# Folding once more over the sequence: even and odd output rows from batch 2 on, in a fused attention and Fourier-mixing kernel

## The chip, the cores and the metric

The kernel runs on one core of a Trainium2 chip. The metric is device microseconds of one execution. TensorE is called PE in the profile, its weight loads PEld, VectorE DVE, ScalarE ACT, GpSimd POOL, and the queue of SyncE SP.

## The reference

Inputs are q, k, v of 8 batches x 12 heads x 448 tokens x 64, and two weights of 768 x 3072 and 3072 x 768, all fp32. Cut to what matters:

```
scores = (1/8) * q @ k^T                 # per batch and head
attn   = max(scores, 0)**2 / 448
x      = attn @ v                        # 8 x 448 x 768 with the heads side by side
mixed  = real(fft(fft(x, axis=1), axis=2))    # over 448 tokens, then over 768 channels
u      = x + mixed
un     = (u - mean(u)) / sqrt(var(u) + 1e-6)  # over the channels
out    = u + max(un @ w1, 0) @ w2
```

## The kernel before

Each batch goes through attention, Fourier mixing, normalization and the feed-forward product (FFN). All of it is written as generators that yield an engine, an estimated duration and what they wait for; a planner (`Streams.run`, L93) takes the step that can start first by its estimates, and so writes a fixed order of instructions for each engine. Semaphores between the engines are put in afterwards, from what each instruction reads and writes. An engine that is later on the chip than in the plan makes the others wait; nothing is reordered at run time.

**Attention** (`attention`, L568) makes the scores of one head pair and quarter of the keys (L645), ACT takes the relu (L670), DVE or ACT squares it (L682, L685), and four such quarters times v give `x` transposed: 128 channels by 448 tokens in PSUM (L627). There are six such blocks m = 0..5 per batch.

**Folding** (`fold`, L489). `leave` scales a block into SBUF as bf16 in two halves: tokens 0..223 from column 0 of `xTc[m]`, and tokens 447..224 backwards from column XH + 1 (XH = 256). So the sum and the difference of the two halves (L535, L537; 225 columns each) are what the cosine and the sine of the transform over the tokens need: each half of the output rows follows from 225 folded tokens in place of 448. Block m and block m + 3 are then combined in the same way over the channels (L546, L549, 450 columns each) into `Bs` and `As`. Each `leave` also starts a DMA transpose (`turn_x`, L555) on SP that gives `xn`, x with tokens on the partitions.

**Mixing** (`mix`, L1096; `mix_rows`, L925). The folded blocks are the stationary side of the channel products with a cosine and sine table `chan` (L1112): folded tokens in two chunks TC of 128 and 97, each 12 matmuls of 193 columns, so 24 per batch. ACT and DVE copy the result to `pc` (L1128). Then the products over the tokens make output rows in two half batches SC, 0..127 and 128..239 (`ch`): for each of cosine and sine two matmuls of 385 columns, one per chunk, accumulate in PSUM (L933), four per half batch. Their sum and difference (L942, L944) give the output row s and the mirrored row 448 - s.

```
for t in range(2):
    for i, (n0, n1) in enumerate(TC):
        nc.tensor.matmul(pq[:n, t, 0:KN], lhsT=seq[:n1 - n0, t, i, s0:s1],
                         rhs=pcs[i][0][:n1 - n0, t, 0:KN], start=(i == 0), stop=(i == 1))
```

Rows and mirrored rows get x added (L960, L962, on DVE and POOL), statistics (L969), and normalization to `un` (L985, L988). `store_rows` (L1012) writes u and un to DRAM: the rows by a plain DMA on SP, the mirrored rows by an indirect DMA on POOL with the row numbers in `back`. `turns` (L1042) fetches `un` transposed for groups of tokens that the FFN takes (384, 512, 384, then nine of 256).

**FFN** (`ffn`, L1275): L1344 is the first product, L1318 and L1316 its relu, L1369, L1395 and L1475 the second product, L1330 the addition to u. PE interleaves FFN work of earlier groups with attention and mixing of later batches; from about 480 us on only FFN is left.

Batches 0 and 1 go partly on paths of their own (`first_tail`, L708; `turn_rows`, L897). `build_dft` (L280) makes the table `seq` over the tokens, `mirrors` (L260) a reversal matrix and the row numbers, on POOL.

Of the kernel before, what the change touches and what calls it, by code (L numbers as in the profile page):

```python
# [140 lines left out]
def mm(n):  # L141
    return n / 2400 + 0.006
# [22 lines left out]
def kernel(  # L165
# [9 lines left out]
    nc = tc.nc  # L175
# [52 lines left out]
    rev = const.tile([128, 128], BF16, name="rev")  # L228

    back = [const.tile([128, 1], mybir.dt.int32, name=f"back{i}") for i in range(2)]  # L230
    warm = work.tile([128, 512], BF16, name="warm", tag="warm", bufs=1)
    xTc = [const.tile([128, 2 * XH], BF16, name=f"xT{m}") for m in range(MC)]

    drow = const.tile([128, 8], FP32, name="drow")
    early_hid = work.tile([128, 6 * KH], FP32, name="early", tag="hT", bufs=1)
# [22 lines left out]
            nc.gpsimd.memset(x[:, XH + NS:2 * XH], 0.0)  # L258

    def mirrors():  # L260
        nc.gpsimd.memset(rev, 0.0)
# [11 lines left out]
    seq = const.tile([128, 2, 2, SX], BF16, name="seqm")  # L273
    nseq = work.tile([128, 2, SX], BF16, name="nseq", tag="qs", bufs=1)
    chan = [const.tile([128, 2, 2 * KH], BF16, name=f"chan{m}") for m in range(3)]

# [39 lines left out]
            dft_ready.t = chan_ready[m].t = e + LATENCY["DVE"]  # L316


    GRP = 4 * R * HG * Dh * 4
    loads = [[None] * 3 for _ in range(B * NG)]  # L320
    ready = [[Cell() for _ in range(3)] for _ in range(B * NG)]
# [6 lines left out]
    def load_group(i, which=(0, 1, 2)):  # L328

        b, g = divmod(i, NG)  # L330
        hs = slice(g * HG, (g + 1) * HG)
        for x, (nm, src) in enumerate((("q", q), ("k", k), ("v", v))):
            if x not in which:
                continue
            if b == 0 and x < 2:
                e = yield need("POOL", 0.85)
                t = first_qk[x][:R, g]
            else:
                e = yield need("POOL", 0.85, bufs=[BQ[x] if x == 2 else BQ[x][home(i)]])
                t = work.tile([R, HG, 4 * Dh], BF16, name=f"{nm}n",  # L340
                              tag="vn" if x == 2 else f"{nm}n{home(i)}", bufs=3 if x == 2 else 1)
            nc.gpsimd.dma_start(out=t, in_=src[b, hs].rearrange("h (p j) d -> p h (j d)", j=4))  # L342
            loads[i][x] = t.rearrange("p h (j d) -> p j h d", j=4)

            ready[i][x].t = sch.dma(e, GRP, 360e3, "sw") + (1.5 if g else 0.0, 3.0, 14.0, 7.0)[min(b, 3)]
            if i == 0 and x == 1:
                yield need("POOL", 0.7)
                make_identity(nc, ident)
            if i == 0 and x == 2:
                e = yield need("POOL", 1.1)  # L350
                dft_indices()
                indices_ready.t = e + LATENCY["POOL"]
            if i == 2 and x == 2:
                yield need("POOL", 0.75)
                pads()
            if i == NG + 1 and x == 1:
                yield need("POOL", 1.8)
                mirrors()


# [128 lines left out]
    def fold(b, m, F, av, give, av_end):  # L489
# [3 lines left out]

        def leave():

            xa = x[:, 0:HS].rearrange("q (p j) -> q p j", j=4), at[:, 0:R // 2]
            xb = x[:, XH + 1:XH + NS].rearrange("q (p j) -> q p j", j=4), at[:, R - 1:R // 2 - 1:-1, ::-1]
            if b == 0:
                t = yield need("DVE", 2 * dve(HS) + 2 * dve2(NS), [av_end], [BX[m]] + ([BA[m]] if m < 3 else []))
                for out_, in_ in (xa, xb):  # L500
# [1 line left out]
            else:  # L502
                yield need("PE", 0.0, [av_end - LATENCY["PE"]])
                en = "ACT" if sooner(av_end, "ACT", 2 * act(HS), "DVE", 2 * dve(HS)) else "DVE"
                bufs = [BX[m]] + ([BA[m]] if m < 3 else [])
# [25 lines left out]
        f = work.tile([128, 2, NS], BF16, name="fold", bufs=1,  # L531
                      tag=f"diff{m - 3}" if b == 0 and m >= 3 else f"fold{min(m, 3)}")
        if not one:
            e1 = yield need("DVE", dve2(NS), [e1])
        nc.vector.tensor_tensor(f[:, 0, :], x[:, 0:NS], x[:, XH:XH + NS], op=ALU.add)  # L535
# [3 lines left out]
        if b == 0:  # L539
            first_folds.append(f)  # L540
            f_ready[m].t = e1 + LATENCY["DVE"]
        elif m >= 3:
            i = m - 3
            e1 = yield need("DVE", (2 if one else 1) * dve2(2 * NS))
            t = work.tile([128, 2, NS], BF16, name="diff", tag=f"diff{i}", bufs=1)
# [3 lines left out]
            nc.vector.tensor_tensor(F[i], F[i], f, op=ALU.add)  # L549
            As[b].append(F[i])  # L550
            ab_ready[b][i].t = e1 + LATENCY["DVE"]

    xn_taken = [Cell() for _ in range(B)]

# [153 lines left out]
    def first_tail(pcs):  # L708
# [180 lines left out]
        yield from unload(3, "DVE")  # L889
        yield from copy(3, 1, "DVE")  # L890
        tail[0] = 2
        sch.add(turn_rows(uns[0][1], max(t_un[1]), 128, rev[:, 63:127], 0, 64, "DVE", second_un[0]), (1, 1))


# [30 lines left out]
    def mix_rows(b, ch, pcs):  # L925

        s0, s1 = SC[ch]
        n = s1 - s0
        e = yield need("PE", 4 * mm(KN), [pcs[0][1], pcs[1][1]], [BS, BTS])
        pq = BS.take()  # L930
        for t in range(2):
            for i, (n0, n1) in enumerate(TC):
                nc.tensor.matmul(pq[:n, t, 0:KN], lhsT=seq[:n1 - n0, t, i, s0:s1],  # L933
                                 rhs=pcs[i][0][:n1 - n0, t, 0:KN], start=(i == 0), stop=(i == 1))
        if ch == 1:
            BPC.free.append(e)
        e = yield need("ACT", act(KN), [e + LATENCY["PE"]])
# [71 lines left out]
        yield need("SP", 0.0, made_un)  # L1009
        un_ready[b][ch].t = max(c.t for c in made_un)  # L1010

    def store_rows(ch, top, bot, us, nbytes, t, cells):  # L1012

        get = lambda u: u() if callable(u) else u
        s0, s1 = SC[ch]
        w = min(128, HS - s0)
# [5 lines left out]
        nc.gpsimd.indirect_dma_start(  # L1022
            out=bot, out_offset=bass.IndirectOffsetOnAxis(ap=back[ch][:s1 - s0], axis=0),
            in_=get(us[1])[:s1 - s0], in_offset=None)
        cells[2 * ch + 1].t = sch.dma(e, w * D * nbytes) + 1.0

    def u_store(b, ch, us, ut, freed):
        yield from store_rows(ch, utop[b], ubot[b], us, 4, ut, u_stored[b])
        yield need("SP", 0.0, freed)
        for i in range(2):  # L1030
            t = max(u_stored[b][2 * ch + i].t, freed[i].t)
            BU[i][side(b, ch)].free.append(t)
            if b == ONE - 1 and ch == 0:
                u_left[i].t = t

    def n_store(b, ch, t):
        yield from store_rows(ch, ntop[b], nbot[b], [lambda i=i: uns[b][2 * ch + i] for i in range(2)], 2,
                              t, n_stored[b])
        if b > 0:
            BUN[0].free.append(n_stored[b][2 * ch + 1].t)  # L1040
# [55 lines left out]
    def mix(b):  # L1096
# [5 lines left out]
            pps = [(pp, c.t + LATENCY["PE"]) for pp, c in zip(first_pps, first_chan)]  # L1102
        else:
            A, Bm = As[b], Bs[b]
            for n0, n1 in TC:
                n = n1 - n0
                e = yield need("PE", 12 * mm(KH), ab_ready[b] + [dft_ready], [BS])
                pp = BS.take()
                for t in range(2):
                    for kp, Y in enumerate((A, Bm)):  # L1110
                        for m in range(3):
                            nc.tensor.matmul(pp[:n, t, kp * KH:(kp + 1) * KH], lhsT=Y[m][:, t, n0:n1],  # L1112
                                             rhs=chan[m][:, t, kp * KH:(kp + 1) * KH],
                                             start=(m == 0), stop=(m == 2))
                pps.append((pp, e + LATENCY["PE"]))
        for m in range(3):
            BA[m].free.append(e)
        for (n0, n1), (pp, t) in zip(TC, pps):
            n = n1 - n0
# [438 lines left out]
    with tc.manual_schedule():  # L1558
# [11 lines left out]
        sch.add(attentions(), (3, 3))  # L1570
        sch.add(warming(), (9, 9))
        sch.add(weight_sums(), (6, 6))
        sch.add(turns(), (1, 1))
        for slot in range(6):
            sch.add(outputs(slot), (4, 0))
# [32 lines left out]
```

## Time and profile before

| | |
|---|---|
| median of 3 runs | 588.73 us (588.59 to 589.23) |
| profiled execution | 588.36 us, span 586.6 us |
| busy PE, DVE, ACT, POOL | 574.5, 411.2, 324.9, 131.0 us |
| granted TensorE clock | 1.0 throughout |
| channel products L1112 | 24 per batch; batches 2 to 7 start at 159, 214, 279, 339, 401 and 460 us |
| row products L933 | 8 per batch, in two sets of four |

The span is what the profiler saw between the first and the last instruction; the rest of the 588.36 us lies around it. Matmuls are pipelined: the duration of one is longer than the distance between two starts, and it is the distance that counts for throughput. In a group of the page, what follows the bar is its busy time and the mean duration of one, then the idle time of its engine just ahead of them and what ended it.

### The profile page before, as it was taken

Reading aid. Unit: us, or ns where it says so; the run is one execution under the profiler, and the core shown is the slowest. Engines: PE = TensorE matmul, PEld = TensorE weight load, DVE = VectorE, ACT = ScalarE, POOL = GpSimd, SP = SyncE. Lnnn points to the kernel's source line nnn. Section 1 sums busy time; section 2 is a strip of 40 time slices with the busy share of each in tenths; the row PEclk is TensorE's granted clock in tenths of the full one; section 3 lists DMA queues with packets and bytes.
Section 4 is the critical chain, followed back from the end, with each engine's and each line's share of the span. In section 5 each row is a group of like instructions: output and inputs, shape, how many; then the busy total and the mean of one; then the engine's idle time right before and its main releaser. Section 6 shows DMA issues by size and latency. Waiting matters only on the chain.

```text
span 586.6 us, 11549 instructions
## 1 busy us (share of the span) xinstructions
PE 574.5 (98%) x4493; PEld 366.8 (63%) x4498; DVE 411.2 (70%) x979; ACT 324.9 (55%) x501; POOL 131.0 (22%) x181
## 2 busy tenths in 40 slices
PE   8999999999999999999999999999999999999997
PEld 6566556544455465556757677567576786868684
DVE  5977677986688959787897778777887682222222
ACT  5967772787767568655738447466485261404040
POOL 8433021411224114211231124210230120000000
PEclk9999999999999999999999999999999999999999
DMA  9999999787959995999659967885472153121211
GB/s 128 207 210 228 217 209 141 183 123 98 179 101 212 187 143 176 158 153 165 105 146 194 166 147 183 147 124 109 143 184 60 50 186 114 41 85 48 73 37 54
DMA packets 133494, 82.30 MB, mean 140 GB/s; under 512 B 77504, under 2 KB 128608, under 8 KB 133440
## 3 DMA queue, kind: packets, MB, share of 16 engines
q0 software_dynamic: 40320, 34.07, 37.6%
q1 hardware_dynamic: 93120, 47.50, 37.0%
q8 instruction: 35, 0.57, 0.4%
q14 instruction: 19, 0.16, 0.1%
HBM read 62.91 MB, written 26.69 MB: 153 GB/s over the span
## 4 chain that ended last, share of the span: by engine, by line
PE 87%; DVE 6%; ACT 3%; DMA 2%; issue 1%; SPq 1%; POOL 0%; DVEq 0%; ACTq 0%; POOLq 0%
PE psF L1344 35%; PE psF L1475 25%; PE psS L645 6%; PE psF L627 5%; PE psF L1395 4%; PE psF L1369 4%; PE psS L1112 2%; ACT sq L670 2%; DMA qkT<-qkr 2%; PE psS L933 2%; DVE sq L685 1%; PE psS L627 1%; PE psS L732 1%; SPq L1262 1%; PE psS L1087 1%
## 5 line engine op out<-in xcount | busy, mean ns | idle before, releaser
L1344 PE MATMUL psF<-unT,w 128*128 128x256 bf16 (+2 forms) x1723 | 229.6, 290 | 1.9 <-ACT unT L907 0.9
L1344 PEld LDWEIGHTS <-w 128*128 128x128 bf16 x1728 | 165.7, 98 | 62.5 <-issue 13.1
L670 ACT ACTIVATE sq<-psS 112x896 bf16<-112x896 f32 x192 | 163.1, 917 | 60.3 <-PE psS L645 56.8
L1318 ACT ACTIVATE hT<-psF 128x512 bf16<-128x512 f32 (+3 forms) x172 | 86.8, 519 | 109.5 <-PE psF L1344 107.3
L685 DVE TENSOR_TENSOR sq<-sq 112x896 bf16<-112x896 bf16 x173 | 106.7, 634 | 15.8 <-ACT sq L670 14.2
L1475 PEld LDWEIGHTS <-hT 128*128 128x128 bf16 x792 | 76.4, 98 | 54.1 <-issue 5.5
L1330 DVE TENSOR_TENSOR o<-psF,o 128x384 f32<-128x384 f32 x92 | 51.0, 554 | 46.2 <-PE psF L1475 41.4
L1475 PE MATMUL psF<-w,hT 128*128 128x384 bf16 x462 | 81.2, 326 | 0.6 <-DVE o L1330 0.6
L645 PE MATMUL psS<-qkT 64*128 64x448 bf16 (+1 forms) x384 | 51.2, 358 | 2.4 <-ACT sq L670 0.8
L342 POOL DMA_DIRECT2D vn<-in_v_dram x24 | 17.2, 716 | 105.1 <-PE psS L645 100.7
L627 PE MATMUL psF<-sq,vn 112*64 112x448 bf16 x328 | 38.8, 359 | 0.0
L512 DVE TENSOR_SCALAR xT<-psF 128x224 bf16<-128x224 f32 x62 | 21.4, 386 | 24.8 <-PE psF L627 23.4
L960 POOL TENSOR_TENSOR u<-tp,xn 128x385 f32<-128x385 f32 (+1 forms) x14 | 13.6, 973 | 103.6 <-DVE tp L942 81.9
L1475 PE MATMUL psF<-wsum,hT 128*128 128x384 bf16 x198 | 34.8, 326 | 0.0
L645 PEld LDWEIGHTS <-qkT 64*128 64x128 bf16 (+1 forms) x384 | 15.9, 102 | 29.4 <-issue 22.6
L342 POOL DMA_DIRECT2D qn<-in_q_dram x21 | 15.4, 733 | 73.7 <-DVE qkr L435 46.7
L627 PEld LDWEIGHTS <-vn 112*64 112x64 bf16 x384 | 17.6, 109 | 21.1 <-issue 12.7
L969 DVE BATCH_NORM_STATS2 stats<-u 128x6 f32<-128x384 f32 (+1 forms) x56 | 28.7, 540 | 0.3 <-POOL u L960 0.3
L988 ACT ACTIVATE un<-u,nmr,rstd 128x768 bf16<-128x768 f32 (+1 forms) x23 | 23.1, 1024 | 9.3 <-DVE nmr L975 8.3
L1369 PE MATMUL psF<-w,hT 128*128 128x384 bf16 x144 | 24.9, 326 | 0.0
L1395 PE MATMUL psF<-w,hT 128*128 128x384 bf16 x144 | 24.7, 326 | 0.2
L1457 DVE TENSOR_TENSOR s<-hT 128x768 bf16<-128x768 bf16 x11 | 6.1, 555 | 25.7 <-ACT hT L1318 25.5
(148 smaller groups left out, 621.8 us busy)
## 6 DMA issues: line engine op xcount, KB each, us to landing
out_dram<-o SPq DMA_DIRECT2D x56, 192.0 KB
vn<-in_v_dram POOLq DMA_DIRECT2D x24, 224.0 KB, 5.8
qn<-in_q_dram POOLq DMA_DIRECT2D x21, 224.0 KB, 7.9
kn<-in_k_dram POOLq DMA_DIRECT2D x21, 224.0 KB, 6.1
w<-in_moe_w_ch_dram POOLq DMA_DIRECT2D x12, 384.0 KB, 14.6
w<-in_moe_w_ch_dram POOLq DMA_DIRECT2D x4, 1152.0 KB
utop<-u SPq DMA_DIRECT2D x8, 384.0 KB
o<-utop SPq DMA_DIRECT2D x16, 192.0 KB
```

What stands on the lines that cost most here:

```text
L342: nc.gpsimd.dma_start(out=t, in_=src[b, hs].rearrange("h (p j) d -> p h (j d)", j=4))
L627: nc.tensor.matmul(av[h * Dh:(h + 1) * Dh, 0:S], lhsT=vn[:, c, h0 + h, :], rhs=sq[:, h, :], start=(c == 0), stop=(c == 3))
L645: nc.tensor.matmul(sc[:wide, h, 0:S].rearrange("k (c q) -> k c q", c=4), lhsT=flat[ps, k0:k0 + wide], rhs=qT[ps, m % 2], start=True, stop= ...
L670: nc.scalar.activation(r, sc[:R, :, 0:S], AF.Relu)
L685: nc.vector.tensor_tensor(r, r, r, op=ALU.mult)
L969: nc.vector.bn_stats(stats[:n, hf, :], u[:n, hf * (D // 2):(hf + 1) * (D // 2)])
L1318: nc.scalar.activation(hs, ps, AF.Relu)
L1330: nc.vector.tensor_tensor(o, pc[:, 0:DH], o, op=ALU.add)
L1344: nc.tensor.matmul(ph[:, i * N:(i + 1) * N], lhsT=w1_sb[m][hf][:, (jj + i) * 128:(jj + i + 1) * 128], rhs=unT[:, m, 0:N], start=(m == 0), ...
L1369: nc.tensor.matmul(pc[:, 0:DH], lhsT=block(j, c), rhs=w2(j, hf), start=(j == 0), stop=(j == JC - 1))
L1395: nc.tensor.matmul(pc[:, 0:DH], lhsT=block(2 * i + k, c), rhs=weights[i], start=(start and i == 0), stop=(i == KP - 1), skip_group_check=True)
L1475: nc.tensor.matmul(pc[:, 0:DH], lhsT=lhs[i], rhs=rhs[i], start=(start and i == 0), stop=(i == KP - 1), skip_group_check=True)
```

## The change

From batch 2 on (PAR = 2) `leave` writes each half with even tokens first and odd tokens behind them. `halves` replaces the folds: it waits for three blocks m, takes sum and difference over all three at a time (EV = 113 columns each for even and odd tokens), and folds each of these once more, columns 0..56 against 112..56 read backwards (EH = 57): the sum serves the even output rows, the difference the odd ones. The combination of m and m + 3 then runs over all of it in two operations of 1368 columns. In `mix` the stationary side of the channel products is 114 columns (57 for the even, 57 for the odd tokens), one set of 12 matmuls for the sums and one for the differences. In `mix_rows` a half batch is the even or the odd rows, 113 and 112 of them, and each needs one matmul for cosine and one for sine. `halve`, run once, makes the smaller table from `seq` with a selection matrix `order`; two memsets in batch 2 clear a pad column. The stores write every second row. Several tiles share homes: three blocks m lie in one tile, `seq` lies in a work buffer that the folds use later.

```
+    PAR, EV = 2, 113
+    EH = EV // 2 + 1
...
+    xT3 = [const.tile([128, 3, 2 * XH], BF16, name=f"xT{k}") for k in range(2)]
+    xTc = [xT3[m // 3][:, m % 3] for m in range(MC)]
...
+    def halve():
+        yield need("SP", 0.0, [tail_left])
+        e = yield need("PE", mm(2 * SX), [], [BS])
+        pt = BS.take()
+        for t in range(2):
+            nc.tensor.matmul(pt[:2 * EH, t, 0:SX], lhsT=order[0][:EV, 0:2 * EH], rhs=seq[:EV, t, 0, :],
+                             start=True, stop=True)
+        e = yield need("DVE", 1.1, [e + LATENCY["PE"]], [BQR])
+        half_seq[0] = work.tile([128, 2, 2, EV], BF16, name="seqh", tag="warm", bufs=1)
+        nc.vector.tensor_copy(half_seq[0][:2 * EH].rearrange("p t o s -> p t s o"),
+                              pt[:2 * EH, :, 0:2 * EV].rearrange("p t (s o) -> p t s o", o=2))
...
     def fold(b, m, F, av, give, av_end):
...
+        if b >= PAR:
+            x_gone[b].append(gone)
+            sch.add(leave(), (0, 0))
+            if m % 3 == 2:
+                sch.add(halves(b, m // 3), (3, 3))
+            return
...
+    def halves(b, k):
+        x = xT3[k]
+        xa, xb = (x[:, :, at:at + 256].rearrange("q m (o e) -> q m o e", o=2)[:, :, :, 0:EV] for at in (0, XH))
+        e1 = yield need("DVE", dve2(6 * EV) + 0.1 * (b == PAR), x_gone[b][3 * k:3 * k + 3] + [seq_left], [BFS])
+        if b == PAR:
+            nc.vector.memset(x[:, :, EV - 1:EV], 0.0)
+        f = work.tile([128, 3, 2, 2, EV + 1], BF16, name="folds", tag="seqm", bufs=1)
+        nc.vector.tensor_tensor(f[:, :, 0, :, 0:EV], xa, xb, op=ALU.add)
+        e1 = yield need("DVE", dve2(6 * EV))
+        nc.vector.tensor_tensor(f[:, :, 1, :, 0:EV], xa, xb, op=ALU.subtract)
+        f = f.rearrange("q m t o e -> q (m t) (o e)")
+        low = f.rearrange("q c (o e) -> q c o e", o=2)[:, :, :, 0:EH]
+        high = f[:, :, 0:2 * EV].rearrange("q c (o e) -> q c o e", o=2)[:, :, :, EV - 1:EH - 2:-1]
+        for w, op in enumerate((ALU.add, ALU.subtract)):
+            e1 = yield need("DVE", dve2(12 * EH), [], [(BFA, BFB)[k]] if w == 0 else [])
+            if w == 0:
+                Y = work.tile([128, 2, 6, 2, EH], BF16, name="fold", tag=("foldA", "foldB")[k], bufs=1)
+            nc.vector.tensor_tensor(Y[:, w], low, high, op=op)
+        if k == 0:
...
+            return
+        first, second = (y.rearrange("q w c o e -> q (w c o e)") for y in (firsts[b], Y))
+        e1 = yield need("DVE", dve2(24 * EH))
+        t = work.tile([128, 24 * EH], BF16, name="diff", tag="seqm", bufs=1)
+        nc.vector.tensor_tensor(t, first, second, op=ALU.subtract)
+        e1 = yield need("DVE", dve2(24 * EH))
+        nc.vector.tensor_tensor(first, first, second, op=ALU.add)
...
     def mix_rows(b, ch, pcs):
...
-        n = s1 - s0
-        e = yield need("PE", 4 * mm(KN), [pcs[0][1], pcs[1][1]], [BS, BTS])
+        n = s1 - s0 if b < PAR else EV - ch
+        e = yield need("PE", (4 if b < PAR else 2) * mm(KN), [pcs[0][1], pcs[1][1]] + [half_ready] * (b >= PAR),
+                       [BS, BTS])
         pq = BS.take()
         for t in range(2):
+            if b >= PAR:
+                nc.tensor.matmul(pq[:n, t, 0:KN], lhsT=half_seq[0][:2 * EH, t, ch, 0:n],
+                                 rhs=pcs[t ^ ch][0][:2 * EH, t, 0:KN], start=True, stop=True)
+                continue
...
     def store_rows(b, ch, top, bot, us, nbytes, t, cells):
...
-            nc.sync.dma_start(out=top[s0:s0 + w, :], in_=get(us[0])[:w])
+            nc.sync.dma_start(out=top[s0:s0 + w, :] if b < PAR else top[ch::2, :], in_=get(us[0])[:w])
...
     def turns():
-                deps = n[1::2] if half else n[0:3:2][int(r0 >= 128):1 + int(r0 + w > 128)]
+                deps = n[half::2]
...
     def mix(b):
-            for n0, n1 in TC:
-                n = n1 - n0
+            for w, (n0, n1) in enumerate(TC):
+                n = n1 - n0 if b < PAR else 2 * EH
...
-                            nc.tensor.matmul(pp[:n, t, kp * KH:(kp + 1) * KH], lhsT=Y[m][:, t, n0:n1],
+                            nc.tensor.matmul(pp[:n, t, kp * KH:(kp + 1) * KH], lhsT=Y[m][:, t, n0:n1] if b < PAR else Y[m][:, w, t],
```

More of the change, by code (lines that the diff above doesn't have):

```diff
@@ L230 @@
     back = [const.tile([128, 1], mybir.dt.int32, name=f"back{i}") for i in range(2)]
+    back2 = [const.tile([128, 1], mybir.dt.int32, name=f"backe{i}") for i in range(2)]
+    order = [None]
     warm = work.tile([128, 512], BF16, name="warm", tag="warm", bufs=1)
-    xTc = [const.tile([128, 2 * XH], BF16, name=f"xT{m}") for m in range(MC)]
+    xT3 = [const.tile([128, 3, 2 * XH], BF16, name=f"xT{k}") for k in range(2)]
+    xTc = [xT3[m // 3][:, m % 3] for m in range(MC)]
     drow = const.tile([128, 8], FP32, name="drow")
@@ L260, in mirrors @@
     def mirrors():
+        order[0] = work.tile([128, 128], BF16, name="order", tag="qkr0", bufs=1)
         nc.gpsimd.memset(rev, 0.0)
@@ L271, in mirrors @@
         nc.gpsimd.tensor_copy(back[1], v[:, 0:1])
-    seq = const.tile([128, 2, 2, SX], BF16, name="seqm")
+        for i in range(2):
+            nc.gpsimd.iota(back2[i], pattern=[[0, 1]], base=HS - i, channel_multiplier=-2)
+        nc.gpsimd.memset(order[0], 0.0)
+        for i in range(2):
+            n = EH - i
+            nc.gpsimd.affine_select(out=order[0][:, i * EH:i * EH + n], in_=order[0][:, i * EH:i * EH + n],
+                                    compare_op=ALU.not_equal, fill=1.0, base=-i, pattern=[[-2, n]],
+                                    channel_multiplier=1)
+        nc.gpsimd.tensor_scalar(order[0][:, EH - 1:EH], order[0][:, EH - 1:EH], 0.5, None, op0=ALU.mult)
+    SEQ = 4 * SX
+    seq_home = work.tile([128, SEQ + 464], BF16, name="seqm", tag="seqm", bufs=1)
+    seq = seq_home[:, 0:SEQ].rearrange("p (t a s) -> p t a s", t=2, a=2)
+    half_seq, seq_left, tail_left, half_ready = [None], Cell(), Cell(), Cell()
     nseq = work.tile([128, 2, SX], BF16, name="nseq", tag="qs", bufs=1)
@@ L316, in build_dft @@
             dft_ready.t = chan_ready[m].t = e + LATENCY["DVE"]
+    def halve():
[9 more added lines that the diff above has]
+                              pt[:2 * EH, :, 0:2 * EV].rearrange("p t (s o) -> p t s o", o=2))
+        BS.give(pt, e)
+        BQR.free.append(e)
+        half_ready.t = e + LATENCY["DVE"]
     GRP = 4 * R * HG * Dh * 4
@@ L356, in load_group @@
             if i == NG + 1 and x == 1:
-                yield need("POOL", 1.8)
+                yield need("POOL", 3.6)
                 mirrors()
@@ L530, in fold @@
             e1 = yield need("DVE", 2 * dve2(NS), [e1])
-        f = work.tile([128, 2, NS], BF16, name="fold", bufs=1,
-                      tag=f"diff{m - 3}" if b == 0 and m >= 3 else f"fold{min(m, 3)}")
+        if m % 3 == 0 and (b == 0 or m == 0):
+            trio[:] = [work.tile([128, 3, 2, NS], BF16, name="fold", tag="foldB" if m else "foldA", bufs=1)] + trio[:1]
+        f = seq_home[:, SEQ:SEQ + 2 * NS].rearrange("q (t n) -> q t n", t=2) if b and m >= 3 else trio[0][:, m % 3]
         if not one:
@@ L551, in fold @@
             ab_ready[b][i].t = e1 + LATENCY["DVE"]
+    x_gone, trio, firsts = [[] for _ in range(B)], [], [None] * B
+    BFA, BFB, BFS = Bufs(1), Bufs(1), Bufs(1)
+    def halves(b, k):
[17 more added lines that the diff above has]
+        if k == 0:
+            BFS.free.append(e1)
+            firsts[b] = Y
+            return
[5 more added lines that the diff above has]
+        nc.vector.tensor_tensor(first, first, second, op=ALU.add)
+        BFB.free.append(e1)
+        for y, home in ((first, As), (t, Bs)):
+            y = y.rearrange("q (w m t e) -> q w m t e", w=2, m=3, t=2)
+            home[b][:] = [y[:, :, m] for m in range(3)]
+        for c in ab_ready[b]:
+            c.t = e1 + LATENCY["DVE"]
     xn_taken = [Cell() for _ in range(B)]
@@ L891, in first_tail @@
         tail[0] = 2
+        tail_left.t = max(first_un[i].t for i in range(4))
         sch.add(turn_rows(uns[0][1], max(t_un[1]), 128, rev[:, 63:127], 0, 64, "DVE", second_un[0]), (1, 1))
@@ L934, in mix_rows @@
                                  rhs=pcs[i][0][:n1 - n0, t, 0:KN], start=(i == 0), stop=(i == 1))
+        if b == PAR - 1 and ch == 1:
+            seq_left.t = e + LATENCY["PE"]
         if ch == 1:
@@ L1036, in n_store @@
     def n_store(b, ch, t):
-        yield from store_rows(ch, ntop[b], nbot[b], [lambda i=i: uns[b][2 * ch + i] for i in range(2)], 2,
+        yield from store_rows(b, ch, ntop[b], nbot[b], [lambda i=i: uns[b][2 * ch + i] for i in range(2)], 2,
                               t, n_stored[b])
@@ L1117, in mix @@
             BA[m].free.append(e)
+        if b >= PAR:
+            BFA.free.append(e)
+            BFS.free.append(e)
         for (n0, n1), (pp, t) in zip(TC, pps):
[L1119 removed]
+            n = n1 - n0 if b < PAR else 2 * EH
             en, copy = ("ACT", nc.scalar.copy) if n0 == 0 else ("DVE", nc.vector.tensor_copy)
@@ L1572 @@
         sch.add(weight_sums(), (6, 6))
+        sch.add(halve(), (3, 3))
         sch.add(turns(), (1, 1))
```

28 lines of the change are left out of this document (19 added, 9 removed).

## The prediction

> **What bounds the kernel now.** I read the busy totals and the 40 slices first, then the chain of work that ended last, then the waits of TensorE (PE) from 60 to 480 us, and at last the groups and the timeline of the lines that the change touches.
>
> ```profile
> span 586.6 us, 11549 instructions
> PE 574.5 (98%) x4493; PEld 366.8 (63%) x4498; DVE 411.2 (70%) x979; ACT 324.9 (55%) x501; POOL 131.0 (22%) x181
> ...
> PE   8999999999999999999999999999999999999997
> ...
> DVE  5977677986688959787897778777887682222222
> ...
> PE 87%; DVE 6%; ACT 3%; DMA 2%; issue 1%; SPq 1%; POOL 0%; DVEq 0%; ACTq 0%; POOLq 0%
> ```
> PE is busy in every slice and holds 87% of the chain. DVE is at 60 to 90% until about 480 us and then nearly free. So a cycle of PE saved anywhere shortens the run, if PE has the next instruction ready.
>
> ```profile
> PE psF L1344 <- ACT unT L907: 0.9, 1, 0.9
> PE psF L1475 <- DVE o L1330: 0.6, 1, 0.6
> PE psS L645 <- DVE pc L1128: 0.6, 1, 0.6
> PE psF L1344 <- DVE xT L512: 0.5, 1, 0.5
> ...
> PE psS L1112 <- DVE fold L549: 0.2, 1, 0.2
> ```
> These are PE's waits between 60 and 480 us (total, times, longest): with two of 0.2 us left out, about 3.2 us, each at a different place. PE's queue is a fixed list that a planner wrote, so any engine that is late against the plan shows as such a wait. The channel products (L1112) wait 0.2 us for the folds.
>
> **The change part by part** (times from the profiled execution: 588.36 us, of which 586.6 are the span; the median is 588.73, so I add the sum to both alike).
>
> Row products, L933. In batches 2 to 7 each half batch needs 2 matmuls of 385 columns in place of 4: 4 fewer per batch, 24 in all. Their price is read from start to start:
>
> ```profile
> 99.41 0.82 PE L933 MATMUL psS<-pc,seqm 128*128 128x385 bf16 x4
> 100.08 1.14 PE L1369 MATMUL psF<-w,hT 128*128 128x384 bf16 x6
> ```
> Four take 100.08 - 99.41 = 0.67 us, 0.167 each (the 0.33 of a single one is latency that overlaps). 24 x 0.167 = 4.0 us off PE. All of it lies on the path.
>
> Channel products, L1112. Still 24 matmuls of 193 columns per batch; only the stationary side changes, from 128 and 97 columns to twice 114. The timeline has 24 of them in 2.00 us, 83 ns each, with 128 and with 97 columns alike. Could the weight load of 114 columns set the pace?
>
> ```profile
> L1112 PEld LDWEIGHTS <-fold 128*97 128x97 bf16 x42 | 4.1, 124 | 0.0
> ...
> L1112 PEld LDWEIGHTS <-fold 128*128 128x128 bf16 x42 | 3.8, 98 | 1.2 <-DVE fold L549 0.4
> ...
> L933 PEld LDWEIGHTS <-seqm 128*112 128x112 bf16 x14 | 1.8, 131 | 0.6
> ```
> ```profile
> 44.90 0.33 PE L736 MATMUL psS<-ident,xT 128*112 128x128 bf16 x3
> 45.06 0.33 PE L732 MATMUL psS<-pc,seqm 128*112 128x384 bf16 x1
> ```
> A load of 112 columns lasts 131 ns, longer than 98 for a full 128, but L736 runs three matmuls of 128 columns behind 112-column loads in 45.06 - 44.90 = 0.16 us, 53 ns each. Loads are pipelined too, and 83 ns leaves them room: I take 0. [...]
>
> New on PE: `halve()` sends 2 matmuls of 240 columns; between the 83 ns of 193 columns and 109 ns of 256 (L1344) that is 0.2 us. Its DVE copy of 452 elements out of PSUM costs about 0.6 us (L942: 385 elements, 0.55). In the order as built it stands near 54 us, between squares that PE awaits; with the copy hidden it is 0.2, with none of it hidden 0.8. I take 0.5, since the PE waits that the profile shows before 64 us are for ACT and DVE.
>
> Folds on DVE, per batch. Removed: 12 of 225 elements and 6 of 450. Added: 4 of 678, 4 of 684 (one input read backwards, in rows of 57) and 2 of 1368.
>
> ```profile
> L535 DVE TENSOR_TENSOR fold<-xT 128x225 bf16<-128x225 bf16 x48 | 13.3, 276 | 1.8 <-ACT xT L509 0.5
> ...
> L549 DVE TENSOR_TENSOR fold<-fold 128x450 bf16<-128x450 bf16 x21 | 8.3, 394 | 0.5
> ```
> The squares (L685, 896 elements) last 0.634 us, so from 450 to 896 elements is 240 ns: 0.54 ns an element over 0.15 us. Before: 12 x 0.274 + 6 x 0.392 = 5.6 us. After: 4 x 0.52 + 4 x 0.52 + 2 x 0.89 = 5.9 us. As DVE has some 20% idle there, 0.3 us a batch costs nothing by itself. What is unknown is the rate of the backward and odd rows: no bf16 row of the trace reads backwards. Backward fp32 has no penalty (L962 on DVE, 383 elements, shortest 0.543; L960 forward, 385, shortest 0.546), but that is 1.03 ns an element over 0.15 us anyway. So a small fold is 0.52 to 0.85 us (684 x 1.03 + 150 ns). I take 0.52, since the forward bf16 rows of odd length 225 already have it. [...]
>
> The wait of L1112 moves: the last chain from `leave` to the channel products was 2 x 0.274 + 2 x 0.392 = 1.3 us and becomes 4 x 0.52 + 2 x 0.89 = 3.9 us. The planner knows this and puts L1112 later in PE's list, with feed-forward products before it. That cover holds to the end: the last L1112 (batch 7) starts at 460 us, and the first group with rows of batch 7 (3072) at 524 us.
>
> A new wait on DVE, in batch 2 alone: two memsets of the pad column wait for the DMA transposes of the two m before. They are issued one leave (5 to 7 us) earlier, and an issue takes 1.2 us on SP (L561; longest 3.1). DVE's queue behind it holds squares. Between 0 and 3 us; I take 0.2 on PE, as the transposes should have landed.
>
> The mirrors on POOL grow by six small operations, each 0.13 to 0.3 us by its rows (iota 0.13, select 0.29): 1.4 us ahead of the first weight loads. POOL already waits 6.1 us for DMA between those, so 0; without that cover 1.4. The stores write every second row, with the same bytes in rows of the same length, and SP's program has no more entries: 0. Transposes of normalized rows now need both half batches; only the groups that start at 2048 and 2560 end in a first 128 rows. The half batches of batch 5 are 5 us apart (343 and 348), and group 2048 starts at 384 us: hidden; without that cover 5 us once.
>
> The planner's list changes too. As built, visits to attention (scores, values) rise from 86 to 89 and 11 squares go from DVE (0.634) to ACT (0.954), which at 55% has room. Coming from scores to feed-forward costs about 0.1 us (six L645 at 103.10, next at 103.77, 0.67 against 3 x 0.19), so three visits with both halves cost about 0.4.
>
> Sum: -4.0 + 0.2 + 0.3 (halve on PE and its copy) + 0.2 + 0.4 = -2.9 us, with PE's other waits as large as now. 588.73 - 2.9 = **585.8 us** (profiled execution 585.5).
>
> **The rivals.**
> *The new list waits more.* The waits sit by chance where ACT, DVE and DMA miss the plan; the list is new from batch 2 on. If their 3.2 us double, the saving is gone: 585.8 + 3.2 = 589.0. For it: squares, leaves and long folds share one DVE queue at 80%. Against it: fewer, longer folds follow the plan no worse, and PE still has feed-forward work between.
>
> *Backward or odd rows run at one element a cycle* (the slower side). Each small fold is 0.33 us longer; two backward ones stand between the last leave and L1112: 0.67 us a batch, 6 x 0.67 = 4.0, so 589.8; with all four, 8.0, so 593.8. That ends slower as soon as any of it adds to the lateness of the squares in the same queue. The plan doesn't know it, and L1112's 0.2 us of waits shows that it is placed about when the folds end. It decides from 0.5 us a batch not hidden. Against it: the forward 225 rows.
>
> *Weight loads set the pace.* Without any overlap of loads 131 ns would stand in place of 83; half way, 107, the 144 channel matmuls lose 24 ns each, 3.5 us: 589.3. Against it: L736's 53 ns. [...]
>
> *Waits vanish.* One wait per batch in place of six, and a lighter DVE: of the 3.2 us most could go, 583.
>
> **How the numbers follow.** Forecast 0.58 (584 to 587.4); more waits 0.17 (587.6 up, beyond 589.9 in 0.04 of it); slow rows 0.10 (588 to 594); paced loads 0.04; waits vanish 0.11 (582 to 584). About 0.2% (1.2 us) is what a measurement of this kernel tells from no change, so faster means below 587.5: 0.58 + 0.11 + 0.02 of the paced loads, partly hidden, = 0.71. Same, to 589.9: 0.13 of the waits, 0.02 of the loads, 0.02 of the slow rows = 0.17. Slower: 0.04 + 0.08 = 0.12. The range, 583.2 to 589.3, leaves out those 0.12 and about half of the vanished waits.
>
> **What would show it.** Right: the row products of batches 2 to 7 as two matmuls 0.167 us apart; channel matmuls still 83 ns apart with loads of about 131 ns; small folds near 0.52 us and large near 0.89; PE's waits from 60 to 480 us near 3 us; busy PE shorter by about 3.5. Wrong: small folds at 0.85 us with PE waiting for them at L1112 in each batch (slow rows); waits doubled at unrelated places (new list); channel matmuls over 90 ns apart (loads); DVE idle for a DMA in batch 2.

## The result, and the profile after

The changed kernel takes 687.06 us (median of 6, 684.71 to 692.38) against 588.34 us for the kernel before on the same chip (6 runs): a ratio of 1.170, interval 1.165 to 1.175. That is 98.7 us slower, where the prediction had 2.9 us faster. The profiled execution took 686.53 us, 684.6 of them the span.

The page of the changed kernel (busy totals, slices in tenths, chain by engine and by line):

```profile
span 684.6 us, 11457 instructions
...
PE 594.1 (87%) x4476; PEld 371.7 (54%) x4476; DVE 408.0 (60%) x929; ACT 331.2 (48%) x503; POOL 153.4 (22%) x190
...
PE   8999999999748999479988699599689936999997
...
PEclk9999999999969899799998999899989977999999
...
PE 42%; DMA 28%; issue 16%; DVE 4%; POOL 4%; ACT 4%; SPq 2%; POOLq 0%; DVEq 0%; ACTq 0%
PE psF L1445 20%; DMA ubot<-u,backe 16%; PE psF L1576 10%; DMA nbot<-un,backe 7%; PE psF L1470 3%; PE psS L734 3%; PE psF L716 3%; ACT sq L759 2%; DMA qkT<-qkr 2%; DMA unT<-ntop 1%; DMA ntop<-un 1%; DMA o<-ubot 1%; POOL u L1057 1%; POOL u L1059 1%; DVE sq L774 1%
```

PE is still full for the first ten slices. From slice 11 on, which begins at 171 us with the first scatter of batch 2, it has holes, and the granted clock is at 0.5 in stretches that begin in the holes or behind them (mean 0.945). DMA holds 28% of the chain in place of 2%, and two lines name it: the scatters of the mirrored rows, `ubot<-u,backe` and `nbot<-un,backe`, 23% of the span. They are the indirect stores of `store_rows` (L1120).

What PE waited for between 60 and 480 us (total, times, longest), the largest and the one that the prediction watched:

```profile
PE psF L1576 <- DVE o L1431: 17.9, 6, 10.1
PE psF L716 <- DVE o L1431: 14.2, 1, 14.2
PE psF L1445 <- DVE xT L553: 6.6, 1, 6.6
...
PE psS L1210 <- DVE fold L634: 0.4, 1, 0.4
```

PE waits for DVE, and yet DVE is less busy than before. How one of these waits arises is seen in the timelines of POOL, DVE and PE (start, duration, in brackets the idle time before and what ended it):

```profile
173.58 2.43 POOL L1120 DMA_INDIRECT ubot<-u,backe  x1 [0.32 <-POOL u L1059]
195.24 0.90 POOL L1057 TENSOR_TENSOR u<-tp,xn 112x385 f32<-112x385 f32 x1 [19.23 <-DMA ubot<-u,backe]
```
```profile
196.18 0.56 DVE L1066 BATCH_NORM_STATS2 stats<-u 112x6 f32<-112x384 f32 x1 [14.70 <-POOL u L1057]
```
```profile
198.25 1.70 PE L716 MATMUL psF<-sq,vn 112*64 112x448 bf16 x8 [14.24 <-DVE o L1431]
```

The even half batch's scatter is issued at 173.58 us. POOL may not write the odd half's mirrored rows over the same buffer until it has landed, 19 us later. DVE stands for 14.7 us at the statistics of these rows with the additions of the FFN queued behind it, and PE, which waits for one of those additions, has nothing to do for 14.24 us. The DMA issues of the changed kernel (count, median us to landing; before, `ubot<-u,back` took 5.1 and `nbot<-un,back` 4.4):

```profile
ubot<-u,backe POOLq DMA_INDIRECT x12, 16.7
nbot<-un,backe POOLq DMA_INDIRECT x12, 9.2
```

The medians mix the two halves: the even ones of u, 113 rows, landed 20.0 to 22.5 us after their issue, the odd ones, 112 rows, after 9.7 to 13.4 us; those of n after 11.7 to 21.6 and 2.8 to 6.7 us. In the packets of the trace, the 113 rows of 3072 bytes of the scatter at 173.58 us went as 56 packets of 6144 bytes and one of 3072, one after another over 17.4 us, while 840 packets of 8 bytes went beside them. In the kernel before, the 128 rows of the same scatter, 64 packets of 6144 bytes, were through in 1.8 us, up to 17 of them at once.

### The profile page after: what moved, and what is told of

It is laid out like the page before. It is cut to its first block, busy times and chain, and to the rows that moved or that the text cites. A ratio compares the mean times of both kernels' runs of the same rounds, so it can differ in the third digit from the quotient of the medians.

```text
span 684.6 us, 11457 instructions
## 1 busy us (share of the span) xinstructions
PE 594.1 (87%) x4476; PEld 371.7 (54%) x4476; DVE 408.0 (60%) x929; ACT 331.2 (48%) x503; POOL 153.4 (22%) x190
## 4 chain that ended last, share of the span: by engine, by line
PE 42%; DMA 28%; issue 16%; DVE 4%; POOL 4%; ACT 4%; SPq 2%; POOLq 0%; DVEq 0%; ACTq 0%
PE psF L1445 20%; DMA ubot<-u,backe 16%; PE psF L1576 10%; DMA nbot<-un,backe 7%; PE psF L1470 3%; PE psS L734 3%; PE psF L716 3%; ACT sq L759 2%; DMA qkT<-qkr 2%; DMA unT<-ntop 1%; DMA ntop<-un 1%; DMA o<-ubot 1%; POOL u L1057 1%; POOL u L1059 1%; DVE sq L774 1%
## 5 line engine op out<-in xcount | busy, mean ns | idle before, releaser
L1445 PE MATMUL psF<-unT,w 128*128 128x256 bf16 (+2 forms) x1728 | 238.9, 298 | 36.9 <-ACT hT L1419 17.1
L1445 PEld LDWEIGHTS <-w 128*128 128x128 bf16 x1728 | 169.7, 100 | 103.7 <-issue 37.3
L774 DVE TENSOR_TENSOR sq<-sq 112x896 bf16<-112x896 bf16 x162 | 98.6, 623 | 20.7 <-ACT sq L759 19.6
L1576 PE MATMUL psF<-w,hT 128*128 128x384 bf16 x462 | 83.7, 333 | 3.5 <-DVE hT L1417 3.5
L1066 DVE BATCH_NORM_STATS2 stats<-u 112x6 f32<-112x384 f32 (+2 forms) x56 | 29.1, 546 | 62.1 <-POOL u L1057 52.0
L716 PE MATMUL psF<-sq,vn 112*64 112x448 bf16 x312 | 38.7, 372 | 14.2 <-DVE o L1431 14.2
L1057 POOL TENSOR_TENSOR u<-tp,xn 112x385 f32<-112x385 f32 (+2 forms) x14 | 12.8, 912 | 170.1 <-DVE tp L1039 86.8
L1069 ACT ACTIVATE std<-mv,eps_t 112x1 f32<-112x1 f32 (+2 forms) x28 | 8.2, 295 | 67.7 <-DVE mv L1067 56.1
L1085 ACT ACTIVATE un<-u,nmr,rstd 113x768 bf16<-113x768 f32 (+2 forms) x20 | 20.1, 1022 | 23.2 <-DMA nbot<-un,backe 12.7
L1417 DVE TENSOR_SCALAR hT<-psF 128x512 bf16<-128x512 f32 (+3 forms) x38 | 20.4, 549 | 16.2 <-PE psF L1445 15.6
L771 ACT ACTIVATE sq<-sq 112x896 bf16<-112x896 bf16 x30 | 28.5, 954 | 0.5
```

The source lines that it names most:

```text
L716: nc.tensor.matmul(av[h * Dh:(h + 1) * Dh, 0:S], lhsT=vn[:, c, h0 + h, :], rhs=sq[:, h, :], start=(c == 0), stop=(c == 3))
L771: nc.scalar.activation(r, r, AF.Square)
L774: nc.vector.tensor_tensor(r, r, r, op=ALU.mult)
L1066: nc.vector.bn_stats(stats[:n, hf, :], u[:n, hf * (D // 2):(hf + 1) * (D // 2)])
L1445: nc.tensor.matmul(ph[:, i * N:(i + 1) * N], lhsT=w1_sb[m][hf][:, (jj + i) * 128:(jj + i + 1) * 128], rhs=unT[:, m, 0:N], start=(m == 0), ...
L1576: nc.tensor.matmul(pc[:, 0:DH], lhsT=lhs[i], rhs=rhs[i], start=(start and i == 0), stop=(i == KP - 1), skip_group_check=True)
```

## The experiments

Theories at the start. A: a scatter of 113 rows goes through one DMA engine. B: writing every second row is slow. C: the new order and the long folds starve PE.

**1. The scatter cut to 112 rows, the 113th row by a DMA of its own on SP** (changed kernel).

```
+        n = min(n, 112) if b >= PAR else n
...
+        if b >= PAR and ch == 0:
+            e = yield need("SP", 0.1, [t[1]])
+            nc.sync.dma_start(out=bot[0:1, :], in_=get(us[1])[112:113])
```

> The changed kernel with one difference: from batch 2 on the scatter of the even mirrored rows takes 112 rows, and the 113th (token 224) goes by a plain DMA of one row on SP. Theory A (a scatter of 113 rows goes through one DMA engine: in the profile after, 57 data packets one after the other, some 17 us, where 128 rows took about 2 us): scatters land in 5 us again, PE waits fall back to a few us, and the time is that of my sum, 583 to 589 us. Theory B (writing every second row is what is slow): the time stays at 680 to 690. Theory C (the new order of work or the longer folds starve PE, and the slow scatter is only where it shows): above 620.

Measured: 595.37 us (ratio 1.012, 1.009 to 1.015). One row less in the scatter takes away 92 of 99 us: A holds for these, and C, which expected more than 620 us, falls. But 7 us remain above before, 9.6 above the prediction, and A's range (583 to 589) is missed. What SP and what PE waited for from 150 to 420 and from 60 to 480 us:

```profile
SPq L1127 <- DMA ubot<-u,backe: 17.9, 5, 4.1
SPq L1127 <- DMA nbot<-un,backe: 17.6, 5, 4.9
```
```profile
PE psS L734 <- DMA qkT<-qkr: 2.9, 1, 2.9
PE psF L1451 <- DVE xT L553: 1.9, 2, 1.3
PE psF L1451 <- DMA unT<-nbot: 1.5, 1, 1.5
```

L1127 is the added row. SP stands there until the scatter has landed, and DMA transposes are queued behind it; two of PE's waits are for such transposes. So this mending has a price of its own.

**2. The old kernel with 113 rows in the scatter** (the other 15 of the 128 by a plain DMA on SP).

```
+        m = 113 if b > 1 and ch == 0 else s1 - s0
...
+            out=bot, out_offset=bass.IndirectOffsetOnAxis(ap=back[ch][:m], axis=0),
+            in_=get(us[1])[:m], in_offset=None)
...
+            nc.sync.dma_start(out=bot[97:112, :], in_=get(us[1])[113:128])
```

> The kernel before with one difference: from batch 2 on the scatter of the first half batch takes 113 of its 128 rows, each still one row apart; the other 15 rows go by a plain DMA on SP, in the wrong order, so rows 97 to 111 of the mirrored halves are changed. Theory A: these scatters need some 20 us in place of 5, and the time rises by 60 to 100 us, to 650 to 690. Theory B and theory C: it stays within 3 us of 588.3, since neither the rows' distance nor the order of PE's work is touched.

Measured: 700.15 us (ratio 1.190), 10 us above A's range. So the loss comes with the old folds, the old order on PE and adjacent rows too, as A says. What the row count costs by itself isn't shown here: SP stood for 97.4 us between 150 and 420 us at the added entry for the other 15 rows, until the scatters had landed. Experiment 5 shows it without such an entry.

**3. The changed kernel, its scatters to adjacent rows.**

```
-            nc.gpsimd.iota(back2[i], pattern=[[0, 1]], base=HS - i, channel_multiplier=-2)
+            nc.gpsimd.iota(back2[i], pattern=[[0, 1]], base=HS - 113 * i, channel_multiplier=-1)
```

> The changed kernel with one difference: the row numbers of the scatters run one apart (224 down to 112, and 111 down to 0) in place of two apart, so the mirrored rows of batches 2 to 7 land in a changed order; row counts stay 113 and 112. Theory A: no change, 680 to 692 us, scatters of 113 rows still near 17 to 20 us. Theory B: back to 583 to 600. Theory C: no change.

Measured: 690.52 us (ratio 1.173, the changed kernel 1.170). B falls.

**4. Scatters alone**, each issued when the last had landed.

> None of the reference is computed: one kernel that issues scatters of 128, 127, 126, 124, 120, 114, 113, 112, 111, 104, 100, 97, 96, 80, 64, 57, 48, 32, 16 and 8 rows, each after the last has landed, three times over: fp32 rows one apart, fp32 rows two apart, bf16 rows one apart. Theory A: counts that share out evenly over the 16 DMA engines (multiples of 16, and of 32 where a packet holds two rows) take 2 to 5 us, 113 takes 17 or more, and other odd counts grow with their rows like one engine, some 0.15 us a row; rows two apart as rows one apart. Theory B: the second series is several times the first.

Measured, from start to start, fp32 rows of 3072 bytes, one row apart (15 of the 20 counts):

| rows | 128 | 127 | 126 | 124 | 120 | 114 | 113 | 112 | 111 | 104 | 100 | 97 | 96 | 57 | 32 |
|---|---|---|---|---|---|---|---|---|---|---|---|---|---|---|---|
| us | 3.50 | 20.84 | 3.70 | 8.87 | 4.00 | 5.60 | 18.66 | 3.67 | 9.77 | 4.04 | 4.33 | 17.12 | 3.46 | 5.20 | 2.64 |

Two rows apart it is the same (113: 18.79); in bf16, half the bytes, 113 rows still take 14.69 against 4.54 for 112. My expectation (16 and its multiples fast, other counts like one engine) was too coarse: 126, 120 and 100 are fast, 124 and 111 in between. The rule that fits all 20 counts takes for the engines at work the largest number up to 16 that divides the row count: 126 = 14 x 9, 100 = 10 x 10, 124 = 4 x 31, 111 = 3 x 37, and 113 is prime.

**5. The changed kernel without the needless row.** The first of the 113 rows is token 448, which does not exist. The scatter starts at the second: 112 rows, no further DMA, the same order on every engine.

```
-            nc.gpsimd.iota(back2[i], pattern=[[0, 1]], base=HS - i, channel_multiplier=-2)
+            nc.gpsimd.iota(back2[i], pattern=[[0, 1]], base=HS - 2 + i, channel_multiplier=-2)
...
-            out=bot, out_offset=bass.IndirectOffsetOnAxis(ap=(back if b < PAR else back2)[ch][:n], axis=0),
-            in_=get(us[1])[:n], in_offset=None)
+            out=bot, out_offset=bass.IndirectOffsetOnAxis(ap=(back if b < PAR else back2)[ch][:n if b < PAR else R], axis=0),
+            in_=get(us[1])[:n] if b < PAR else get(us[1])[n - R:n], in_offset=None)
```

> The changed kernel; its first of 113 even mirrored rows is a dummy (token 448 does not exist), so the scatter starts one row later: 112 rows from partition 1, row numbers shifted by one, for both half batches from batch 2 on. No further DMA, every engine's order of instructions as in the changed kernel. Theory D: what the split scatter still had too much came from its own extra row on SP: SP stood 17.9 + 17.6 us at that entry for the scatter to land, and the transposes queued behind it came late (PE's 2.9 us for qkT and 1.5 us for unT). Then this kernel comes to the prediction's sum, 585.5 to 587, with PE waits of about 3 to 4 us between 60 and 480 us. Theory E: the new order and the folds themselves make PE wait: 592 to 596, with the waits of the split kernel at the same places.

Measured: 588.65 us (12 runs, 586.4 to 594.04) against 588.92 for before (23 runs): ratio 0.9999, 0.998 to 1.002. The instructions of every engine are those of the changed kernel in the same order, so the row count alone makes 98 us of the loss. The extra row on SP was 6.7 of the 9.6 us, so D holds for that part, but the time lies between its range (to 587) and E's (from 592). The sum is still missed by about 3 us, and the runs spread more than those of before (587.72 to 590.53). The timelines of DVE and PE in its profiled run (589.12 us) show a second cause:

```profile
155.15 0.69 DVE L553 TENSOR_SCALAR xT<-psF 128x224 bf16<-128x224 f32 x2 [1.11 <-PE psF L716]
160.19 0.06 DVE L612 MEMSET xT<- 128x3 bf16 x1 [4.35 <-DMA xn<-xT]
160.28 0.52 DVE L614 TENSOR_TENSOR folds<-xT 128x678 bf16<-128x678 bf16 x1
```
```profile
155.72 4.06 PE L1445 MATMUL psF<-unT,w 128*128 128x512 bf16 x18
...
163.38 5.73 PE L1445 MATMUL psF<-unT,w 128*128 128x512 bf16 x18 [2.93 <-DVE hT L1417]
```

The memset of the pad column (L612, batch 2) waits 4.35 us for the DMA transposes of the same tile; folds, squares and a relu stand behind it in DVE's queue, and PE, which awaits the relu, idles 2.93 us. SP issued the last of these transposes here:

```profile
153.44 1.73 SPq L650 DMA_TRANSPOSE xn<-xT  x1
```

Its `leave` had ended at 150.30; SP had other DMAs to issue first, and the memset could start only 6.7 us behind this issue. The 18 matmuls behind the hole take 5.73 us where the same group ahead of it took 4.06: another 1.7 us. The stretch of 6 us that holds them (its length, then busy time of PE, PEld, DVE, ACT and POOL, granted clock, DMA share, GB/s) shows the clock at 0.72:

```profile
162.00:168.00 6.00, 4.62 (x14) 1.80 (x14) 5.97 (x12) 1.92 (x4) 1.54 (x2) 0.72 0.36 37
```

**6. The row products issued twice**, in the kernel of experiment 5.

```
+                for again in range(2):
                     nc.tensor.matmul(pq[:n, t, 0:KN], lhsT=half_seq[0][:2 * EH, t, ch, 0:n],
```

> The kernel of 112 scattered rows, with each of the 24 row products of batches 2 to 7 issued twice (the same result written again; the order of everything else is the same). It measures the term of the prediction's sum for the row products. If PE is the bound throughout: 24 x 0.167 = 4.0 us above the kernel of 112 rows, the prediction's saving. If PE has slack before or behind these products (it would wait anyway): less, down to 0.

Measured: 590.92 us, 2.3 more. Not decisive: in its profiled run the memset waited 2.0 us where its sister waited 4.3, so the same wait disturbs both sides of the comparison.

**7. The pad column cleared early**, ahead of each `leave` of batch 2, when the tile's last transposes (batch 1) have long landed. Otherwise experiment 5.

```
+                if b == PAR:
+                    nc.vector.memset(x[:, EV - 1:EV], 0.0)
                 split = at.rearrange("q p (h o) -> q o p h", o=2)
...
-        if b == PAR:
-            nc.vector.memset(x[:, :, EV - 1:EV], 0.0)
```

> The kernel of 112 scattered rows, with the pad column of batch 2 cleared block by block ahead of each leave (six memsets of one column, on a tile whose last transposes were those of batch 1) in place of the two memsets behind the leaves; everything else in the same order on every engine. Theory F: what is missing from the prediction's saving is the wait of the second of those memsets for the transposes of batch 2 (DVE idle 4.3 us in the profiled run of 112 rows, 2.0 in its sister, PE then idle 2.9 and 0.9 us, and the granted clock at 0.72 for 6 us behind the longer one). Then: no DVE idle for xn, PE's gap at 163 us gone, 584.5 to 586.5. Theory G: the wait only lets another one through, since the folds come late for other reasons, or the new order is the loss: 588 to 589, as with 112 rows.

Measured: 584.63 us (584.15 to 585.93) against 588.98: ratio 0.9928, 0.9912 to 0.9943. F holds, and this version beats both kernels, that of before by 0.7%. All that PE waited for from 60 to 480 us:

```profile
PE psF L1445 <- ACT unT L997: 0.9, 1, 0.9
PE psF L1576 <- DVE o L1431: 0.6, 1, 0.6
PE psF L1445 <- DVE mv L1067: 0.6, 1, 0.6
PE psF L505 <- DVE qkT L510: 0.2, 1, 0.2
PE psF L1445 <- ACT hT L1419: 0.2, 1, 0.2
PE psF L1576 <- DVE hT L1417: 0.2, 1, 0.2
```

That is 2.7 us, where before had 3.2, and no wait is for a DMA.

**8. Its row products issued twice** (the edit of experiment 6 on experiment 7).

> The kernel with early memsets, each of the 24 row products of batches 2 to 7 issued twice as in the run before. It measures the saving of the row products without the disturbance of the memset's wait: 24 x 0.165 = 3.9 to 4.0 us above the kernel with early memsets if PE is the bound wherever these products stand; less if not.

Measured: 589.29 us, 4.7 more by the medians (about 1.3 either way by the two ratios); 3.6 by the profiled spans (586.2 and 582.6), 3.9 by the lowest runs. On PE the products take 7.86 in place of 3.96 us from start to start. Within this spread each saved product is worth its full time.

**9 and 10. Which of the slow scatters costs** (experiment 7 with 113 rows again, in the scatters of `nbot` alone, then of `ubot` alone).

```
+        odd = b >= PAR and ch == 0 and nbytes == 2
...
+            in_=get(us[1])[:n] if b < PAR or odd else get(us[1])[n - R:n], in_offset=None)
```

In experiment 10 the 2 is a 4.

> The kernel with early memsets and 112-row scatters, in which only the scatters of the normalized rows (bf16, into nbot, even rows, one per batch from batch 2) have 113 rows again. Alone, 113 bf16 rows took 14.7 us in place of 4.5. Theory J: the slow scatters cost through the single buffer of mirrored u rows: the odd half's u (POOL L1057) may not be written until the even half's scatter has read it, and what follows (statistics, un, transposes, the FFN's next group) shifts by as much. Then the n scatters matter little: 586 to 600. Rival K: each slow landing costs alike, wherever it stands: 6 of the 12 landings, half of the 100 us, 625 to 640.

> As the run before, but only the scatters of u (fp32, into ubot, even rows) have 113 rows: alone 18.7 us in place of 3.7. Theory J: most of the 100 us comes back: 650 to 685. Rival K: half of them, 630 to 645.

Measured: 621.62 and 652.57 us, that is 37.0 and 67.9 us above experiment 7, 6.2 and 11.3 per batch. Together they give 104.9, about the whole loss. Neither theory has both sizes. J's range for u (650 to 685) holds, but its cheap n scatters are not cheap (586 to 600 forecast); K, which has the two alike, misses both ranges. Alone a landing is 15.0 us (u) and 10.2 us (n) later with 113 rows than with 112; three quarters and three fifths of it reach the end. The waits that each leaves on POOL, experiment 9 first:

```profile
POOL un L1083 <- DMA nbot<-un,backe: 23.1, 3, 8.1
```
```profile
POOL u L1058 <- DMA ubot<-u,backe: 86.5, 6, 19.8
```

In experiment 9 PE waits for transposes of normalized rows as well (6.3 and 6.2 us, once each).

**11. The rule on new row counts.**

> Scatters alone as before (one after the other has landed), with other row counts. The rule read from the first table: the rows are shared over the largest number of DMA engines, at most 16, that divides the row count, and the time goes with the rows per engine (from the first table: 2.6 to 3.7 us up to 8 rows on each, 4.3 at 10, 5.2 to 5.6 at 19, 8.9 at 31, 9.8 at 37, 17 to 21 at 97 to 127). So, fp32, from start to start: 128 3.5; 125 (5 engines of 25) about 7; 122 (2 of 61) 12; 121 (11 of 11) 4.4; 119 (7 of 17) 5.2; 118 (2 of 59) 12; 117 (13 of 9) 4.0; 112 3.7; 110 (11 of 10) 4.3; 109 (1 of 109) 18.5; 105 (15 of 7) 3.6; 98 (14 of 7) 3.6; 86 (2 of 43) 10.5; 85 (5 of 17) 5.2; 61 (1 of 61) 12; 51 (3 of 17) 5.2; 49 (7 of 7) 3.5; 37 (1 of 37) 9.8; 19 (1 of 19) 5.3; 13 (13 of 1) 2.6. The rival: only counts that leave few rows over when cut into 16 are fast, so 119, 118, 117 (7, 6, 5 left over) are alike and slower than 109 is not.

Measured (fp32, one row apart, 15 of the 20 counts), with the engines that the rule gives:

| rows | 125 | 122 | 121 | 119 | 118 | 117 | 110 | 109 | 105 | 86 | 85 | 61 | 49 | 37 | 19 |
|---|---|---|---|---|---|---|---|---|---|---|---|---|---|---|---|
| engines | 5 | 2 | 11 | 7 | 2 | 13 | 11 | 1 | 15 | 2 | 5 | 1 | 7 | 1 | 1 |
| us | 6.90 | 11.88 | 4.57 | 6.21 | 11.60 | 3.71 | 4.31 | 18.61 | 3.60 | 9.34 | 5.68 | 11.95 | 3.71 | 8.76 | 5.50 |

Most come within 0.5 us of what the rule foretold (119 is 1.0 us later, 86 and 37 are 1.2 and 1.0 earlier). The packets agree: where each engine has an odd number of rows, one packet of a single row is left over per engine, and the trace has 5, 11, 7, 13 and 1 of them at 125, 121, 119, 117 and 109 rows. The packets of 8 bytes fit too: there is one for every pair of rows on a working engine and every engine of the 16 that has none (840 = 56 x 15 at 113 rows, 132 = 12 x 11 at 125, 72 = 8 x 9 at 119, 12 = 4 x 3 at 117). With 16 packets for every two fp32 or three bf16 rows, or part of them, that one engine has, and 16 more a scatter, the rule gives 12304 for the 60 scatters of experiment 4, and its trace has 12304 in their queue. The rival falls: 118 with 6 rows over takes 11.60, 117 with 5 over 3.71.

## Why the prediction was wrong

**The step that failed** is "The stores write every second row, with the same bytes in rows of the same length, and SP's program has no more entries: 0." The rows are as long as before, SP has no more entries, and the bytes are even fewer (225 rows scattered per batch in place of 240); what is wrong is the 0. What changed is the number of rows in a scatter, 128 to 113, and with it how many packets went at once: up to 17 in 1.8 us with 128 rows, one after another over 17.4 us with 113. It is worth 98 us: 687.06 with 113 rows, 588.65 with 112 (experiment 5). No row of the trace of before shows an odd row count, so by the prediction's own manner the term should have had bounds from both sides; it had a price of nothing, no cover and no rival. Alone, a scatter of 128 rows took 3.50 us and one of 113 rows 18.66 (experiment 4).

**The second step** is the memsets of batch 2: "Between 0 and 3 us; I take 0.2 on PE, as the transposes should have landed." They had not: DVE stood 2.0 to 4.3 us. The prediction counted 1.2 us for the issue and nothing for SP's other entries ahead of it, nor for the landing: in the changed kernel the last of these transposes was issued 2.5 us behind the end of its `leave` and landed 5.0 us after that (in experiment 5, 3.1 and about 6.7 us). Its list of signs did name this one, "DVE idle for a DMA in batch 2". Between experiments 5 and 7 the term is 4.0 us, outside its own range. In the profiled run of experiment 5, PE's hole of 2.9 us is followed by a lower clock (0.72 over 6 us), which cost 1.7 us more; the prediction counted the wait and not what follows it.

**The terms that held**, read in the kernel of experiment 7, from each matmul's start to the next:
- Row products: 9.43 us before, 5.29 after, so -4.1 (predicted -4.0). Experiment 8 shows that all of it reaches the end, to within its spread.
- Channel products: 14.33 before, 14.04 after (predicted no change), 83 ns apart behind loads of 131 ns. The paced loads fall.
- Folds: 0.52 us small and 0.87 large (predicted 0.52 and 0.89). The backward ones (L624) take 0.52 where the rival of slow rows had 0.85, so it falls:

```profile
L624 DVE TENSOR_TENSOR fold<-folds 128x684 bf16<-128x684 bf16 x24 | 12.2, 520 | 0.1
L616 DVE TENSOR_TENSOR folds<-xT 128x678 bf16<-128x678 bf16 x12 | 6.1, 510 | 0.0
...
L632 DVE TENSOR_TENSOR diff<-fold 128x1368 bf16<-128x1368 bf16 x6 | 5.2, 868 | 0.1
L634 DVE TENSOR_TENSOR fold<-fold 128x1368 bf16<-128x1368 bf16 x6 | 5.2, 864 | 0.0
```

- `halve`: 0.34 us on PE (0.2 predicted). Its copy took 2.2 us and not 0.6, and still cost nothing that can be seen (before 64 us PE waited 4.5 us in the kernel before and 3.6 in this one): 0.3 too much there.
- More attention visits: scores and values took 88.2 us before without the gaps and 88.1 after, 0.4 too much.
- Waits of the list: 2.7 us against 3.2. The rival of a list that waits more falls for this list, and the both-half dependency is hidden (no wait for a DMA into `unT`; the 0.9 us for ACT's `unT` was there before).

So with both defects mended the kernel gains 4.3 us by the medians, 4.0 by the profiled spans, where the sum had 2.9: the copy (0.3), the visits (0.4) and, with its wait gone, the memset (0.2) did not cost what the sum has for them. The saving was real and the chance of slower, 0.12, rested on the wrong mechanisms.

## What to carry to other kernels

When a change alters a tile's shape, ask what every instruction that carries the new shape does with it, the DMAs first, and run alone what no row of the trace shows: the bytes may be nearly the same and the time five times as long (3.67 us for 112 rows, 18.66 for 113). Choose row counts of scatters that divide well (112, not 113), and do not mend an odd row with an entry in a queue that others stand behind. A wait that comes once can be worth more than its own length if PE goes idle (2.9 us here, and 1.7 more): count the slower clock behind it.

## What the runs showed of the hardware

- A scatter's time, alone and in fp32 (experiment 4), goes with the rows on each engine as the rule above counts them: about 2.6 to 4.0 us up to 9 rows, 8.9 at 31, 18.7 at 113, 20.8 at 127. One row more or less can be a factor of five or six (112 rows 3.67 us, 113 rows 18.66; 127 rows 20.84, 128 rows 3.50). The issue on POOL lengthens too, from 0.98 us for 110 rows to 2.30 for 109 (experiment 11).
- Holes of PE of 2.9 us (experiments 1 and 5) came with a lower granted clock behind them: 0.83 in the 10 us from 340 us in experiment 1, 0.72 in the 6 us from 162 us in experiment 5, 1.7 us lost in either (10 x 0.17, 6 x 0.28). In the trace of the changed kernel each of the 12 holes of 2.7 to 14.2 us has its stretch at half the clock, 3.4 us or two to four times as long, which begins in the hole or up to 0.7 us behind it (at most 1.2 us in experiment 5, where the clock is at 1.00 again from 168 us); the holes of 1.3 to 1.6 us there and in experiment 1 have none.
- A DVE copy of 452 fp32 elements out of PSUM into bf16, whose output is written in an inner run of two elements that do not lie side by side, took 2.20 us (experiment 7); a copy of 384 elements out of PSUM into bf16 without such a run (L997) took 0.55. Which of its differences causes this was not tried.
